# Pairing the layer 1 activations, splitting a weight load, and moving a weight load and the end of a linear-attention kernel

## The chip, the cores and the metric

The kernel runs on one core of one Trainium2 chip. The metric is device time in microseconds (us), the median of several runs. The engines are named as in the profile: PE is TensorE (PEld its weight loads), DVE is VectorE, ACT is ScalarE, POOL is GpSimd, SP is SyncE, which here issues DMAs. A label such as L177 is line 177 of that kernel's file; the change shifts the lines a little, so L178 of the kernel before is L177 of the changed one.

## The reference, cut to what matters

```python
def phi(x):                                   # elu(x) + 1
    return np.where(x > 0, x, np.exp(x) - 1.0) + 1.0
q_p, k_p = phi(q), phi(k)                     # q, k, v: 8 batches x 8 heads x 576 x 64, fp32
kv  = np.einsum('bhsd,bhse->bhde', k_p, v)
z   = np.sum(k_p, axis=2)
num = np.einsum('bhsd,bhde->bhse', q_p, kv)
den = np.einsum('bhsd,bhd->bhs', q_p, z)[..., None] + 1e-06
x   = (num / den) as 4608 tokens x 512
h   = x @ w_in                                # 512 x 2048     "layer 1"
out = (h - np.tanh(h)) @ w_out                # 2048 x 512     "layer 2"
```

## The kernel before

The 4608 tokens are cut into nine tiles of 512. In each tile `c`, layer 1 makes 16 blocks `fi` of 128 x 512 (four matmuls each), ACT takes the tanh and DVE subtracts it into `gT`; layer 2 then takes 16 steps of four matmuls. The attention of the next batch is threaded between these steps by two tables: `s1[fi]` lists what is emitted after block `fi` of layer 1, and `s2[s]` what is emitted after step `s` of layer 2. Each engine is given its instructions in the order in which they are emitted, and in the traces read here no instruction of DVE, ACT or POOL was seen to overtake another: DVE of the changed kernel, for one, starts `prepare`, which needs nothing of q of batch 1, at 39.17 us, after the second `qp` at 38.50 us that waited for it.

```python
def l1act(fi, h, gT):
    th = mpool.tile([128, 512], F32, name="th")            # mpool: bufs=3
    nc.scalar.activation(th, h, AF.Tanh)
    nc.vector.tensor_sub(gT[:, fi, :], h, th)

def gate(gT, fi):                                          # POOL waits here, then issues loads
    g0 = rpool.tile([1, 1], BF16, name="g0")
    nc.gpsimd.tensor_copy(g0, gT[0:1, fi, 0:1])

# loads, all issued from POOL, fp32 in HBM to bf16 on chip, in this order
...                                                        # q, k, v of batch 0
for g in range(4):
    load_wi(g)                                             # 512 columns of w_in each
load_k(1)
load_wo(0)
load_q(1)
...                                                        # memsets
load_wo(1)
load_v(1)
load_wo(2)
...
# first tile (c == 0): attention of batch 1 beside layer 2
s2[0].append(lambda: a_qphi(1, 0))                         # needs q of batch 1
s2[1].append(lambda: (a_qphi(1, 1), load_q(2), load_wo(3), load_k(2), load_v(2)))
s2[4].append(lambda: a_qT_pe(1, 0, side))                  # transposes of qp on PE
s2[5].append(lambda: a_qT_pe(1, 1, side))
s2[5].append(lambda: (b0_scale_rest(side), prepare()))     # DVE
s2[6].append(lambda: a_kv(1, side))                        # 36 small matmuls on PE
s2[8].append(lambda: a_den(1, side))
s2[9].append(lambda: (num1(), a_split(1)))
s2[11].append(lambda: (spread1(0), a_qphi(2, 0)))          # scales of xT for the next tile
s2[13].append(lambda: (spread1(1), a_qphi(2, 1), a_qT_dma(2)))
s2[15].append(lambda: (a_kphi(2, 0), a_vp(2, 0, nc.gpsimd), a_vp(2, 1, nc.gpsimd)))
...
if c >= 1 and n2 < B:                                      # loads of the batch after next
    s1[0].append(lambda: (gate(gT, 0), load_k(n2), load_q(n2), load_v(n2)))
```

`ps_all` is the memory into which the matmuls write (PSUM), here eight banks of 128 x 512. `side` hands out four of these banks in turn. `b0_scale_rest` does four small matmuls into one of them (the "rest" matmuls), and a DVE multiplication (the "rest scale") that frees the bank; `prepare` is nine small DVE instructions that make selection matrices. From the second tile on, `1/den` takes a way round by HBM: SP writes `rden` to `ds` and reads it back, spread over partitions, as `rdb`; DVE needs `rdb` to write `xT` in layer 2.

## Time and profile before

| | before |
|---|---|
| median of 6 runs beside the changed kernel | 295.31 us (295.28 to 295.72) |
| span of the profiled run (first to last instruction) | 293.7 us |
| PE busy / DVE / ACT | 97% / 63% / 51% |
| mean granted PE clock | 0.997 |
| longest PE wait for a load | 1.70 us, for part 1 of `w_out` |

The prediction below shows the lines of this profile on which it rests. A line of the group view reads: line, engine, operation, output <- input, shape, count | busy us in all, mean ns of one | idle time of the engine just before them and what ended it. Two groups are shown here because the change is to halve their number:

```profile
L373 DVE TENSOR_TENSOR gT<-ps_all,th 128x512 bf16<-128x512 f32 x144 | 96.5, 687 | 46.7 <-ACT th L372 46.0
L372 ACT ACTIVATE th<-ps_all 128x512 f32<-128x512 f32 x144 | 85.3, 597 | 48.1 <-PE ps_all L367 42.2
```

Both engines are mostly idle before these instructions, waiting for PE, so they are not what limits the kernel.

### The profile page before, as it was taken

The numbers are of one execution on the slowest core, as the hardware profiler recorded it, in microseconds if no ns is written. First come the engines' busy times: TensorE is split into PE (matmuls) and PEld (weight loads), VectorE is DVE, ScalarE is ACT, GpSimd is POOL, SyncE is SP. The second block draws the span as 40 slices with busy tenths as digits, with TensorE's granted clock in tenths as the row PEclk, the third lists the DMA queues.
The fourth block names the chain that finished last, engine by engine and source line by source line (L and its number), as shares of the span: only waits on it lengthen the run. The fifth ranks groups of instructions, "written<-read, shape, count | busy, mean of one in ns | idle before, by whom it ended". The sixth has DMA issues, their size and how long they took to land.

```text
span 293.7 us, 4685 instructions
## 1 busy us (share of the span) xinstructions
PE 285.4 (97%) x1801; PEld 134.1 (46%) x1801; DVE 183.9 (63%) x326; ACT 150.6 (51%) x233; POOL 34.6 (12%) x55
## 2 busy tenths in 40 slices
PE   8999799999999999999999999999999999999994
PEld 2544364444444444544444445444444444444443
DVE  4759857996578665775578557955780478008600
ACT  4948717766355654555356535752561166136411
POOL 8562030420030002000020003000000000000000
PEclk9999999999999999999999999999999999999998
DMA  7999999897969765957797769787117310130033
GB/s 104 193 205 214 206 206 211 178 186 151 215 119 208 154 142 117 192 120 173 149 152 147 179 138 144 120 203 143 38 34 167 71 37 0 41 85 19 2 71 71
DMA packets 38534, 38.95 MB, mean 133 GB/s; under 512 B 16304, under 2 KB 33264, under 8 KB 37744
## 3 DMA queue, kind: packets, MB, share of 16 engines
q0 software_dynamic: 17008, 18.35, 38.2%
q1 hardware_dynamic: 21424, 20.27, 30.9%
q8 instruction: 14, 0.23, 0.3%
q14 instruction: 8, 0.07, 0.1%
q10 hardware_dynamic: 80, 0.03, 0.0%
HBM read 43.91 MB, written 9.55 MB: 182 GB/s over the span
## 4 chain that ended last, share of the span: by engine, by line
PE 81%; DMA 9%; DVE 5%; POOL 3%; issue 1%; ACT 0%; DVEq 0%; POOLq 0%
PE ps_all L382 39%; PE ps_all L367 35%; DMA w_out_sb<-in_moe_w_out_dram 5%; DMA w_in_sb<-in_moe_w_in_dram 4%; PE ps_all L318 2%; PE ps_all L200 2%; DVE gT L373 1%; PE ps_all L575 1%; DVE xT L360 1%; PE ps_all L277 1%; DVE r L136 1%; DVE kp L137 1%; POOL v L409 1%; PE ps_all L178 1%; DVE qp L137 1%
## 5 line engine op out<-in xcount | busy, mean ns | idle before, releaser
L382 PE MATMUL ps_all<-w_out_sb,gT 128*128 128x512 bf16 x560 | 128.2, 379 | 1.7 <-DMA w_out_sb<-in_moe_w_out_dram 1.7
L367 PE MATMUL ps_all<-xT,w_in_sb 128*128 128x512 bf16 x576 | 128.1, 379 | 0.4 <-DMA w_in_sb<-in_moe_w_in_dram 0.4
L373 DVE TENSOR_TENSOR gT<-ps_all,th 128x512 bf16<-128x512 f32 x144 | 96.5, 687 | 46.7 <-ACT th L372 46.0
L372 ACT ACTIVATE th<-ps_all 128x512 f32<-128x512 f32 x144 | 85.3, 597 | 48.1 <-PE ps_all L367 42.2
L367 PEld LDWEIGHTS <-w_in_sb 128*128 128x128 bf16 x576 | 55.2, 98 | 66.8 <-issue 0.9
L382 PEld LDWEIGHTS <-gT 128*128 128x128 bf16 x560 | 53.9, 98 | 65.9 <-issue 2.1
L388 ACT COPY osb<-ps_all 128x512 f32<-128x512 f32 (+2 forms) x37 | 21.2, 574 | 76.5 <-PE ps_all L382 59.8
L329 DVE TENSOR_TENSOR xT<-ps_all,rdb 128x512 bf16<-128x512 f32 x24 | 16.5, 690 | 14.2 <-PE ps_all L318 14.2
L135 ACT ACTIVATE e<-qraw 128x1152 bf16<-128x1152 bf16 x16 | 18.5, 1163 | 4.6 <-DMA qraw<-in_q_dram 4.6
L137 DVE TENSOR_TENSOR kp<-e,r 128x1152 bf16<-128x1152 bf16 x15 | 12.1, 809 | 12.5 <-ACT e L135 11.6
L135 ACT ACTIVATE e<-kraw 128x1152 bf16<-128x1152 bf16 x15 | 17.4, 1163 | 0.2 <-DMA kraw<-in_k_dram 0.2
L137 DVE TENSOR_TENSOR qp<-e,r 128x1152 bf16<-128x1152 bf16 x16 | 12.1, 758 | 7.9 <-ACT e L135 7.1
L378 POOL COPY g<-gT 1x1 bf16<-1x1 bf16 x5 | 0.9, 179 | 108.4 <-DVE gT L373 108.4
L318 PE MATMUL ps_all<-qT,kz 128*128 128x512 bf16 x28 | 10.1, 379 | 0.0
L434 PE MATMUL ps_all<-zero 128*128 128x512 bf16 x29 | 8.8, 466 | 1.2 <-DVE zero L396 1.2
L136 DVE TENSOR_SCALAR r<-qraw 128x1152 bf16<-128x1152 bf16 x16 | 7.3, 455 | 1.9 <-DMA qraw<-in_q_dram 1.9
L200 PE MATMUL ps_all<-vp,kp 64*128 64x136 bf16 x216 | 7.6, 220 | 0.2 <-DVE kp L137 0.2
L136 DVE TENSOR_SCALAR r<-kraw 128x1152 bf16<-128x1152 bf16 x15 | 7.7, 514 | 0.0
L200 PEld LDWEIGHTS <-kp 64*128 64x128 bf16 x216 | 6.4, 94 | 2.9 <-issue 2.5
L286 DVE RECIPROCAL rden<-den 128x144 f32<-128x144 f32 x7 | 7.4, 1053 | 0.2
L93 POOL DMA_DIRECT2D qraw<-in_q_dram x7 | 5.2, 748 | 14.7 <-DVE r L136 12.3
L93 POOL DMA_DIRECT2D kraw<-in_k_dram x7 | 5.3, 752 | 4.3 <-issue 1.6
(80 smaller groups left out, 105.3 us busy)
## 6 DMA issues: line engine op xcount, KB each, us to landing
out_dram<-osb SPq DMA_DIRECT2D x70, 128.0 KB
rdb<-ds SPq DMA_DIRECT2D x12, 576.0 KB
kraw<-in_k_dram POOLq DMA_DIRECT2D x7, 576.0 KB, 5.9
qraw<-in_q_dram POOLq DMA_DIRECT2D x7, 576.0 KB, 8.0
v<-in_v_dram POOLq DMA_DIRECT2D x7, 576.0 KB, 10.8
w_in_sb<-in_moe_w_in_dram POOLq DMA_DIRECT2D x8, 256.0 KB, 11.7
w_out_sb<-in_moe_w_out_dram POOLq DMA_DIRECT2D x4, 512.0 KB, 14.3
qraw<-in_q_dram POOLq DMA_DIRECT2D x2, 288.0 KB, 4.4
```

The lines of the kernel that those rows point to most:

```text
L93: nc.gpsimd.dma_start(out=t.rearrange("q h i j d -> q (h i) (j d)"), in_=x.rearrange("(n q) x -> q n x", n=4))
L135: return (lambda: nc.scalar.activation(e, x, AF.Exp), lambda: nc.vector.tensor_scalar(r, x, 0.0, 1.0, ALU.max, ALU.add), lambda: nc.vector ...
L136: lambda: nc.vector.tensor_scalar(r, x, 0.0, 1.0, ALU.max, ALU.add),
L137: lambda: nc.vector.tensor_tensor(y, e, r, ALU.min))
L200: nc.tensor.matmul(ps[hg][:, i, :], kp[r, i, j].rearrange("p h d -> p (h d)"), vp[r, i, j, :], start=(j == 0), stop=(j == J - 1))
L318: nc.tensor.matmul(ps, kz[:, p // 2, p % 2, 0:128], qT[:, p % 2, 0:8, p // 2, :], start=True, stop=True)
L329: nc.vector.tensor_mul(xT[:, p, S * b:S * b + 512].rearrange("p (j t c) -> p j t c", j=8, t=4), ps.rearrange("p j (t c) -> p j t c", t=4), ...
L367: nc.tensor.matmul(h, w_in_sb[:, 2 * (p % 2) + p // 2, fi * 128:(fi + 1) * 128], xT[:, p, c * 512:(c + 1) * 512], start=(n == 0), stop=(n ...
L372: nc.scalar.activation(th, h, AF.Tanh)
L373: nc.vector.tensor_sub(gT[:, fi, :], h, th)
L382: nc.tensor.matmul(o, gT[:, fi, i * 128:(i + 1) * 128], w_out_sb[:, fi, :], start=(fi == 0), stop=(fi == NF - 1))
L388: nc.scalar.copy(osb[:, f0:f1], o[:, f0:f1])
```

## The change

The intent is fourfold: fewer instructions on ACT and DVE (activations over two blocks at once from the second tile on), no wait for part 1 of `w_out` (its load goes ahead of q of batch 1, and the work that needs q1 moves to later steps), an earlier first matmul (256 columns of `w_in` in a load of their own), and a shorter end (the last eviction by DVE, its stores over two queues).

```diff
-    mpool = ctx.enter_context(tc.tile_pool(name="mpool", bufs=3))
+    mpool = ctx.enter_context(tc.tile_pool(name="mpool", bufs=2))
+    def l1act2(fi, h, gT):
+        th = mpool.tile([128, 2, 512], F32, name="th")
+        nc.scalar.activation(th, h, AF.Tanh)
+        nc.vector.tensor_sub(gT[:, fi:fi + 2, :], h, th)
 ...
-        nc.scalar.copy(osb[:, f0:f1], o[:, f0:f1])
+        if f0:
+            nc.vector.tensor_copy(osb[:, f0:f1], o[:, f0:f1])
+        else:
+            nc.scalar.copy(osb[:, f0:f1], o[:, f0:f1])
+        last = c == NC - 1 and i == 3          # its second half goes over ACT's queue
 ...
-    for g in range(4):
-        load_wi(g)
+    for f0, n in ((0, 256), (256, 256), (512, 512), (1024, 512), (1536, 512)):
+        load_wi(f0, n)
     load_k(1)
     load_wo(0)
+    load_wo(1)
     load_q(1)
 ...
-    load_wo(1)
     load_v(1)
 ...
-            s2[0].append(lambda: a_qphi(1, 0))
-            s2[1].append(lambda: (a_qphi(1, 1), load_q(2), load_wo(3), load_k(2), load_v(2)))
-            s2[4].append(lambda: a_qT_pe(1, 0, side))
-            s2[5].append(lambda: a_qT_pe(1, 1, side))
-            s2[5].append(lambda: (b0_scale_rest(side), prepare()))
-            s2[6].append(lambda: a_kv(1, side))
-            s2[8].append(lambda: a_den(1, side))
-            s2[9].append(lambda: (num1(), a_split(1)))
-            s2[11].append(lambda: (spread1(0), a_qphi(2, 0)))
-            s2[13].append(lambda: (spread1(1), a_qphi(2, 1), a_qT_dma(2)))
-            s2[15].append(lambda: (a_kphi(2, 0), a_vp(2, 0, nc.gpsimd), a_vp(2, 1, nc.gpsimd)))
+            s2[3].append(lambda: a_qphi(1, 0))
+            s2[4].append(lambda: (a_qphi(1, 1), load_q(2), load_wo(3), load_k(2), load_v(2)))
+            s2[6].append(prepare)
+            s2[7].append(lambda: (b0_scale_rest(side), a_qT_pe(1, 0, side), a_kv(1, side), a_qT_pe(1, 1, side)))
+            s2[9].append(lambda: a_den(1, side))
+            s2[10].append(lambda: (num1(), a_split(1)))
+            s2[12].append(lambda: (spread1(0), a_qphi(2, 0)))
+            s2[14].append(lambda: (spread1(1), a_qphi(2, 1), a_qT_dma(2)))
+            s2[15].append(lambda: a_kphi(2, 0))
 ...                                            # a_vp(2, i), now on DVE, goes to s1[3] of the second tile
-            s1[0].append(lambda: (gate(gT, 0), load_k(n2), load_q(n2), load_v(n2)))
+            s1[1].append(lambda: (gate(gT, 0), load_k(n2), load_q(n2), load_v(n2)))
 ...
-            l1act(fi, h, gT)
+            if c == 0:
+                l1act(fi, h, gT)
+            elif fi % 2:
+                n = dense.order[(dense.n - 1) % 6]
+                l1act2(fi - 1, ps_all[:, n - 1:n + 1, :], gT)
```

More of the change, by code (lines that the diff above doesn't have):

```diff
@@ L105, in load_v, with load_wi @@
         load(b, v_b[b % 2][:, 0:2], v, b == 0)
-    def load_wi(g):
-        f0 = g * (DF // 4)
+    def load_wi(f0, n):
         for h in range(2):
-            nc.gpsimd.dma_start(out=w_in_sb[64 * h:64 * h + 64, :, f0:f0 + DF // 4],
-                                in_=moe_w_in[256 * h:256 * h + 256, f0:f0 + DF // 4].rearrange(
+            nc.gpsimd.dma_start(out=w_in_sb[64 * h:64 * h + 64, :, f0:f0 + n],
+                                in_=moe_w_in[256 * h:256 * h + 256, f0:f0 + n].rearrange(
                                     "(t d) f -> d t f", d=64))
@@ L187, in a_kv, with a_vp @@
             nc.vector.tensor_mul(kz_t[b][:, hg], ps[hg][:, :, 0:160], mask[:, hg])
-    def a_vp(b, i, eng):
-        eng.tensor_copy(vp[:, i, :, 0:128].rearrange("p j (h d) -> p h j d", h=2), v_b[b % 2][:, 0:2, i])
+    def a_vp(b, i):
+        nc.vector.tensor_copy(vp[:, i, :, 0:128].rearrange("p j (h d) -> p h j d", h=2), v_b[b % 2][:, 0:2, i])
     def a_kv_cols(b, banks):
@@ L368, in l1mm @@
                          start=(n == 0), stop=(n == NP - 1))
+    def l1act2(fi, h, gT):
+        th = mpool.tile([128, 2, 512], F32, name="th")
+        nc.scalar.activation(th, h, AF.Tanh)
+        nc.vector.tensor_sub(gT[:, fi:fi + 2, :], h, th)
     def l1act(fi, h, gT):
-        th = mpool.tile([128, 512], F32, name="th")
+        th = mpool.tile([128, 2, 512], F32, name="th")[:, 0, :]
         nc.scalar.activation(th, h, AF.Tanh)
@@ L387, in evac @@
         osb = opool.tile([128, DM], F32, name="osb")
-        nc.scalar.copy(osb[:, f0:f1], o[:, f0:f1])
-        for half, q_ in enumerate((nc.sync, nc.sync if f1 < DM or c < NC - 1 or i < 3 else nc.scalar)):
+        if f0:
[3 more added lines that the diff above has]
+        last = c == NC - 1 and i == 3
+        for half in range(2):
             b, j = divmod(2 * (4 * c + i) + half, J)
-            q_.dma_start(out=out[b * S:(b + 1) * S, f0:f1].rearrange("(p j) m -> p j m", j=J)[:, j, :],
+            (nc.scalar if last and half else nc.sync).dma_start(out=out[b * S:(b + 1) * S, f0:f1].rearrange("(p j) m -> p j m", j=J)[:, j, :],
                               in_=osb[64 * half:64 * half + 64, f0:f1])
@@ L530 @@
             s1[1].append(lambda: a_kphi(2, 1))
+            for i in range(2):
+                s1[3].append(lambda i=i: a_vp(2, i))
         if c >= 1 and n2 < B:
-            s1[0].append(lambda: (gate(gT, 0), load_k(n2), load_q(n2), load_v(n2)))
+            s1[1].append(lambda: (gate(gT, 0), load_k(n2), load_q(n2), load_v(n2)))
             d = 2
@@ L539 @@
             for i in range(2):
-                s2[14 + i].append(lambda i=i: a_vp(n2, i, nc.vector))
+                s2[14 + i].append(lambda i=i: a_vp(n2, i))
         if c == 0:
```

## The prediction

Two of its steps can be read from the profile before. The 1.2 us for the subtraction of a pair: a TENSOR_TENSOR of DVE from `ps_all` and an fp32 tile to bf16 took 415 ns at 128x256 (L264) and 687 ns at 128x512 (L373), so a straight line gives 1231 ns at 128x1024; this is an estimate. And that ACT and DVE do not overtake: in the trace each starts its instructions in the order given, so what waits for a late load holds what stands behind it. POOL likewise issued the load of q of batch 2 only after 12.32 us of waiting for DVE's `r`, and part 3 of `w_out` behind it, at 36.40 and 37.13 us.

> **What bounds the kernel now.** I read the page's busy line first, then who waited for whom, then the timeline. The busy line:
>
> ```profile
> PE 285.4 (97%) x1801; PEld 134.1 (46%) x1801; DVE 183.9 (63%) x326; ACT 150.6 (51%) x233; POOL 34.6 (12%) x55
> ```
>
> TensorE (PE) is the bound; DVE at 63% and ACT at 51% have slack over the whole. What PE waited for (us, times, longest):
>
> ```profile
> PE ps_all L382 <- DMA w_out_sb<-in_moe_w_out_dram: 1.7, 1, 1.7
> ...
> PE ps_all L367 <- DMA w_in_sb<-in_moe_w_in_dram: 0.4, 1, 0.4
> ...
> PE ps_all L200 <- DVE kp L137: 0.2, 1, 0.2
> ```
>
> Only 1.7 us is worth hunting. The chain of waits says the same: from 62.2 us to 289.7 us every piece is PE, a 128x512 matmul each 0.216 us (24 in 5.18). So only the first 62 us and the last 4 can move, and layer-1 activations after 62 us have nothing to give unless they become a wait.
>
> In the first 51 us DMA is saturated; by windows (last column GB/s):
>
> ```profile
> 32.00:34.00 2.00, 2.00 (x11) 0.89 (x10) 2.00 (x4) 0.78 (x2) 0.00 (x0) 1.00 1.24 207
> 34.00:36.00 2.00, 0.44 (x3) 0.10 (x1) 1.27 (x4) 1.76 (x2) 0.00 (x0) 1.00 1.22 208
> ```
>
> Loads land one after another in order of issue. Issue times plus time to landing, issue by issue, give: k of batch 1 at 28.1, w_out 0 at 30.7, q1 33.5, w_out 1 36.1, v1 38.9, w_out 2 41.4, q2 44.3, w_out 3 46.9, k2 49.7, v2 52.5: 2.6 us for 512 KB, 2.8 for 576 KB. The timeline (start, us) around the wait:
>
> ```profile
> 33.55 2.22 ACT L135 ACTIVATE e<-qraw 128x1152 bf16<-128x1152 bf16 x2 [1.23 <-DMA qraw<-in_q_dram]
> ...
> 35.98 0.76 DVE L137 TENSOR_TENSOR qp<-e,r 128x1152 bf16<-128x1152 bf16 x1
> 36.14 1.02 PE L382 MATMUL ps_all<-w_out_sb,gT 128*128 128x512 bf16 x4 [1.70 <-DMA w_out_sb<-in_moe_w_out_dram]
> ...
> 39.41 0.41 DVE L264 TENSOR_TENSOR xT<-ps_all,rdb 128x256 bf16<-128x256 f32 x1
> 39.74 0.70 DVE L481 CAST s<-ident 32x16 f32<-32x16 bf16 x4
> ...
> 39.95 1.66 PE L178 MATMUL ps_all<-v,kp 64*128 64x192 bf16 x36
> ...
> 41.07 0.43 DVE L489 CAST sel<-s 128x512 bf16<-128x512 f32 x1
> ```
>
> q1 is ready for use (qp of both halves) 3.2 us after it lands (33.5 to 36.7). `prepare` (casts to sel) takes 1.76 us on DVE (39.74 to 41.50), here hidden beside the 36 kv matmuls.
>
> [...] 512 rows of 1024 B take 2.57 us, 512 of 1152 B take 2.82. [...] while POOL copies vp (52.6 to 55.4), a DVE instruction of 0.45 us takes 1.40:
>
> ```profile
> 52.97 1.40 DVE L136 TENSOR_SCALAR r<-kraw 128x1152 bf16<-128x1152 bf16 x1
> ```
>
> **The change, part by part.**
>
> *Activations in pairs, from the second tile on.* 128 tanh and 128 subtractions become 64 each. ACT: two of 597 ns become one of about 1.01 us (the 128x1024 copy in the trace took 1.01)[...]. That saves about 64 x 0.18 = 11 us of ACT[...], all of it beside PE: nothing off the time. Risk: from the end of a pair's matmuls to its release is 1.0 + 1.2 = 2.2 us instead of 1.3. Six banks go round in 6 x 0.864 = 5.2 us; a pair takes 1.73 to fill and 2.2 to empty, 3.95 in all, so 1.2 us are left. At the turn to layer 2 the last pair is needed after 14 matmuls, 3.0 us, and ready after 2.2. Both hold, in steady tiles.
>
> *First w_in columns alone.* The first matmuls of layer 1 start at 16.25 after 0.4 us of wait for w_in. Next on PE is the second spread, which starts at 16.77 when DVE's second scale ends at 16.70, whatever w_in does. Gain 0. Cost: the first 512 KB go in rows of 512 B. From 80.3 ns a row and engine at 1024 B (2.57 us / 32) and 88.1 at 1152 B, about 49 ns at 512 B, against 40 for half a row of 1024 B: 64 rows x 9 ns = 0.6 us for all later landings (estimate); I take 0.4.
>
> *w_out 1 ahead of q1.* The queue's bytes are the same. w_out 1 now lands at 33.3 + 0.4, before PE needs it at 34.4: the 1.7 us go. But q1 lands at 36.1 + 0.4. The program's order on each engine then gives (before adding 0.4): steps 4 to 7 of layer 2 run 34.3 to 37.7; the 0.12 us of rest matmuls to 37.85; transposes of q1's first half need qp at 38.1 and end at 38.6; kv needs v1 at 38.9. Its first matmul goes, its second must wait for the bank of the rest matmuls, which is free when DVE has done the rest scale. DVE's order is qp, qp, prepare, rest scale: 36.1 + 3.2 = 39.3, + 1.76 = 41.05, + 0.41 = 41.45. So `prepare`, meant to fill idle DVE time, stands behind the late q1 and in front of what PE waits for: 2.4 us of PE idle. Then kv (1.6) to 43.05 and transposes (0.5) to 43.5, where step 8 starts. Before, step 7 started at 41.54, so step 8 at 42.4: +1.1 us, or +1.5 with the 0.4. PE waits of about 3.0 us replace one of 1.7.
>
> *Turn to the second tile.* The second spread stands three steps before layer 1 instead of four (first: 12 instead of 11; second: 14 instead of 13). Before, spread at 47.41, last xT scale done at 51.74, layer 1 at 51.45 needing it at 52.1: 0.36 us in hand. Now one step of 0.86 fewer is between: about 0.5 us of wait. Then `vp` moves from POOL to DVE (2 x 0.45, behind the second pair). ACT from the end of step 12 (49.5) runs four evictions (2.1), three exp of 1.15 and then tanh, exp, tanh (1.0, 1.15, 1.0), so the second tanh ends at 58.3, the subtraction at 59.5, the first vp copy at 60.0; PE wants it after seven columns at 59.05. Wait about 1.0 us, where there was 0.17. Against that, DVE is no longer held up by POOL's copy (1.7 us in two instructions); that is already in these times.
>
> *End.* The last SP issue goes at about 290.0 instead of 290.53, because the other half of the 384-column piece goes over ACT's queue and DVE does the last eviction. But the ACT queue's piece, issued at 290.01 before, stays where it was, and its packets ended only 0.16 us before SP's last: 0.2 us gained.
>
> *Sum:* 1.1 + 0.4 + 0.5 + (1.0 - 0.2) - 0.2 = +2.6 us, 297.9. After the second tile PE runs without waits, so nothing of it is caught up.
>
> **The rivals.** (1) It gains: the w_out wait goes and q1 is early enough. That makes 295.3 - 1.7 - 0.2 = 293.4. For it: q1's products stand later in the order, so the author gave them room. Against it: q1 moves by 2.6 us in a saturated queue, and DVE's order puts 5.4 us between its landing and the bank that kv wants. (2) Pairs starve PE of banks in every tile: 0.3 us on eight tiles would be +2.4 on top, 300. The 1.2 us in hand and DVE at 63% speak against it. (3) The 2.4 us gap and its neighbours leave PE so idle that the clock is lowered; the 1.7 us gap now does not do it (granted clock 1.00 in all windows)[...]. (4) The waits overlap: a later start of the second tile leaves ACT and DVE to catch up and the 0.5 and 0.8 vanish: 296.6.
>
> **Range and chances.** I shade the sum a little for rival 4 and put 297.6. Low end 295.8: both waits of the turn absorbed and the small rows free. High end 299.2: rivals 2 or 3 in part. 2% is 5.9 us; PE's own work forbids so large a gain, and a loss needs bank starvation in all tiles.
>
> **What would show it.** Right: no PE wait for w_out at 34 us; q1 landing near 36.4; a PE wait of over 2 us at the kv matmuls (line 177), named DVE xT of line 263, near 39 to 42 us; layer 1 of the second tile starting near 52.9 instead of 51.45; a wait for vp (line 189) near 59; from there the PE chain without gaps as before. Wrong: q1 landing before 34.5, the kv matmuls without a wait, or PE waiting for gT (line 373) in tile after tile.

## The result, and the profile after

| | before | after |
|---|---|---|
| median of 6 runs each | 295.31 us | 300.02 us (299.07 to 300.27) |
| ratio | | 1.0152, 95% interval 1.0137 to 1.0167 |
| span of the profiled run | 293.7 us | 298.5 us |
| mean granted PE clock in it | 0.997 | 0.994 |

A ratio in this document is the mean time of one kernel's fast runs over that of the other's in the same rounds, so it is not quite the ratio of the medians. The changed kernel is 1.5% slower, outside the predicted range: 2.4 us above the predicted time and 0.8 us above the top of the range. The loss is real: the slowest of the runs before is 295.72 us and the fastest after is 299.07 us.

The page of the changed kernel, its busy line, its clock in 40 slices of 7.46 us, and the two groups:

```profile
PE 287.7 (96%) x1801; PEld 135.1 (45%) x1801; DVE 175.4 (59%) x265; ACT 139.8 (47%) x168; POOL 33.3 (11%) x55
...
PEclk9999988999999999999999999999999999999999
...
L373 DVE TENSOR_TENSOR gT<-ps_all,th 128x1024 bf16<-128x1024 f32 x64 | 77.9, 1218 | 60.2 <-ACT th L372 60.2
L372 ACT ACTIVATE th<-ps_all 128x1024 f32<-128x1024 f32 x64 | 65.5, 1024 | 58.4 <-PE ps_all L366 48.5
```

ACT is busy 10.8 us less, for 11 us expected, and DVE 8.5 us less: a pair takes 1024 and 1218 ns, where two single ones took 1194 and 1374. PE has the same 1801 matmuls but is busy 2.3 us *more* (287.7 against 285.4). The same work at the same clock should take about as long; the two slices marked 8 in the clock row say where to look, 37 to 52 us.

What PE waited for (us in all, times, longest), and then its timeline in layer 2 of the first tile (start us, us, what, and in brackets the idle time before it and what ended it):

```profile
PE ps_all L177 <- DVE xT L263: 2.6, 1, 2.6
...
PE ps_all L199 <- DVE vp L189: 0.8, 1, 0.8
PE ps_all L317 <- DVE xT L328: 0.6, 1, 0.6
```

```profile
31.14 7.08 PE L387 MATMUL ps_all<-w_out_sb,gT 128*128 128x512 bf16 x32
...
38.99 0.25 PE L177 MATMUL ps_all<-v,kp 64*128 64x192 bf16 x1 [0.16 <-DMA v<-in_v_dram]
41.85 2.02 PE L177 MATMUL ps_all<-v,kp 64*128 64x192 bf16 x35 [2.61 <-DVE xT L263]
...
44.73 2.71 PE L387 MATMUL ps_all<-w_out_sb,gT 128*128 128x512 bf16 x8
```

The wait for `w_out` is gone: 32 matmuls of layer 2 run in one piece where there was a 1.70 us hole. A hole of 2.61 us stands 3 us later, and it is the one predicted. But the eight matmuls after it take 2.71 us; eight of them took 1.90 us in the kernel before. The windows (length, busy us of PE, PEld, DVE, ACT and POOL with counts, granted clock, DMA share, GB/s) tell why:

```profile
40.00:42.00 2.00, 0.15 (x4) 0.15 (x5) 1.89 (x8) 0.00 (x0) 1.89 (x3) 1.00 0.85 95
42.00:44.00 2.00, 2.00 (x38) 1.70 (x35) 0.35 (x2) 0.00 (x0) 0.00 (x0) 0.74 1.19 200
44.00:46.00 2.00, 2.00 (x12) 1.19 (x11) 1.09 (x3) 0.69 (x1) 0.00 (x0) 0.50 1.16 180
46.00:48.00 2.00, 2.00 (x24) 0.84 (x23) 0.14 (x1) 0.00 (x0) 0.00 (x0) 0.90 1.21 202
```

About 1.1 us after the hole PE falls to half clock. In shorter windows the clock reads 0.97 from 42.5 to 43.0 us, 0.50 from 43.0 to 46.0, 0.62 from 46.0 to 46.5 and 1.00 after that, so it is half from 42.97 to 46.38 us. These 3.4 us at half clock leave 1.7 us of work undone. Before, the same windows show 1.00.

Where the 4.8 us of the span came from, by following the start of each stage in both traces:

| stage | after minus before | what was added in the stage before it |
|---|---|---|
| layer 2 of tile 0 starts | +0.3 us | first loads landed 0.2 us later; from -0.1 to +0.8 in the other runs, so not of the change |
| layer 1 of tile 1 starts | +3.1 | -1.70 (`w_out`), +2.61 (kv), +0.16 (v), +1.7 (clock) |
| layer 2 of tile 1 starts | +4.1 | +1.0: waits for the `xT` scales and for `vp` |
| layer 2 of tile 4 starts | +4.2 | nothing but 0.1 |
| layer 1 of tile 5 starts | +5.0 | +0.8: a wait for `rdb` |
| end of the last matmul | +5.0 | nothing |
| end of the span | +4.8 | -0.2: the new end |

The last line of the waits above belongs to tile 4. In the timeline there, DVE stands idle 1.29 us for the broadcast of `1/den`, and PE stands behind it:

```profile
173.75 1.89 DVE L328 TENSOR_TENSOR xT<-ps_all,rdb 128x512 bf16<-128x512 f32 x3 [1.29 <-DMA rdb<-ds]
174.50 0.38 PE L317 MATMUL ps_all<-qT,kz 128*128 128x512 bf16 x1 [0.63 <-DVE xT L328]
```

Why is `rdb` late, from the second tile on, where PE ran without waits before? The gate that opens a tile's loads moved. These are POOL's lines in tile 3, first of the kernel before, then of the changed one:

```profile
115.31 0.18 POOL L378 COPY g<-gT 1x1 bf16<-1x1 bf16 x1 [27.61 <-DVE gT L373]
115.80 0.75 POOL L93 DMA_DIRECT2D kraw<-in_k_dram  x1 [0.31 <-issue]
```

```profile
121.28 0.18 POOL L383 COPY g<-gT 1x1 bf16<-1x1 bf16 x1 [27.61 <-DVE gT L373]
121.77 0.74 POOL L93 DMA_DIRECT2D kraw<-in_k_dram  x1 [0.31 <-ACT th L372]
```

Layer 1 of tile 3 starts at 112.80 us before and at 116.94 us after, 4.1 us later; the loads start 6.0 us later. The gate reads the first block of `gT`, which is now written by the instruction for a pair, so it waits for two blocks of matmuls and for the longer tanh and subtraction. The loads sit 1.8 us deeper in the tile. SP's writes of `rden` to `ds` do not seem to complete until these loads are through: in the ten pairs that I compared (five tiles in each kernel), `rdb` is issued between 0.2 us before and 0.8 us after v of that tile has landed (landing taken as issue plus time to landing), for instance at 158.6 us before (v at 158.1) and 164.4 us after (v at 163.9). In the last tile that needs `rdb`, where no loads run, it is issued 2.4 us after the write of `ds`. SP's lines in tile 4, first before, then after:

```profile
155.05 1.30 SPq L306 DMA_DIRECT2D ds<-rden  x4
158.59 1.13 SPq L309 DMA_DIRECT2D rdb<-ds  x2
```

```profile
159.35 1.30 SPq L305 DMA_DIRECT2D ds<-rden  x4
164.41 1.13 SPq L308 DMA_DIRECT2D rdb<-ds  x2
```

In this tile `rdb` follows the write of `ds` by 3.5 us before and by 5.1 us after. What holds the four writes of 4.5 KB so long is not shown: `rdb` follows v's landing, and no run here took the loads away to prove the cause. Nor is a late issue the whole of the loss: e3 below keeps the moved gate and issues `rdb` in tile 4 as late (5.0 us after the write of `ds`), yet its PE lost only 0.04 us from tile 3 to tile 6. In the changed kernel the broadcast then took 9.3 us to reach DVE, in e3 at most 8.1 us; why that differs is open.

### The profile page after: what moved, and what is told of

It is laid out like the page before. It is cut to its first block, busy times and chain, and to the rows that moved or that the text cites. A ratio compares the mean times of both kernels' runs of the same rounds, so it can differ in the third digit from the quotient of the medians.

```text
span 298.5 us, 4501 instructions
## 1 busy us (share of the span) xinstructions
PE 287.7 (96%) x1801; PEld 135.1 (45%) x1801; DVE 175.4 (59%) x265; ACT 139.8 (47%) x168; POOL 33.3 (11%) x55
## 4 chain that ended last, share of the span: by engine, by line
PE 72%; DMA 17%; DVE 5%; issue 1%; ACT 1%; SPq 1%; POOL 1%; DVEq 0%; POOLq 0%
PE ps_all L366 34%; PE ps_all L387 32%; DMA qraw<-in_q_dram 5%; DMA w_in_sb<-in_moe_w_in_dram 3%; DMA rdb<-ds 3%; PE ps_all L199 2%; DMA out_dram<-osb 2%; DMA kraw<-in_k_dram 2%; PE ps_all L317 2%; DMA ds<-rden 1%; DVE qp L136 1%; DVE xT L359 1%; PE ps_all L276 1%; DVE gT L373 1%; PE ps_all L177 1%
## 5 line engine op out<-in xcount | busy, mean ns | idle before, releaser
L373 DVE TENSOR_TENSOR gT<-ps_all,th 128x1024 bf16<-128x1024 f32 x64 | 77.9, 1218 | 60.2 <-ACT th L372 60.2
L372 ACT ACTIVATE th<-ps_all 128x1024 f32<-128x1024 f32 x64 | 65.5, 1024 | 58.4 <-PE ps_all L366 48.5
L396 ACT COPY osb<-ps_all 128x512 f32<-128x512 f32 (+1 forms) x36 | 20.9, 583 | 73.1 <-PE ps_all L387 49.7
L136 DVE TENSOR_TENSOR kp<-e,r 128x1152 bf16<-128x1152 bf16 x15 | 11.4, 758 | 7.6 <-ACT e L134 6.7
L378 DVE TENSOR_TENSOR gT<-ps_all,th 128x512 bf16<-128x512 f32 x16 | 10.3, 685 | 2.4 <-ACT th L377 1.7
L377 ACT ACTIVATE th<-ps_all 128x512 f32<-128x512 f32 x16 | 9.2, 598 | 4.3 <-PE ps_all L366 3.1
```

What stands on the lines that cost most here:

```text
L136: lambda: nc.vector.tensor_tensor(y, e, r, ALU.min))
L373: nc.vector.tensor_sub(gT[:, fi:fi + 2, :], h, th)
L396: nc.scalar.copy(osb[:, f0:f1], o[:, f0:f1])
```

## The experiments

All kernels were correct. Each had its own runs of the kernel before on the same chip, with medians from 295.02 to 295.29 us.

| label | what it is | median us (runs) | ratio to before |
|---|---|---|---|
| e1_prepare_first | after, `prepare` four steps earlier | 298.36 (6) | 1.0110 |
| e2_spin_in_gap | after, matmuls on zeros in the kv gap | 298.52 (4) | 1.0115 |
| e3_q1_first | after, old order of loads | 296.65 (6) | 1.0054 |
| e5_q1_first_vp_pool | e3, `vp` on POOL as before | 296.28 (4) | 1.0041 |
| e4_pairs_only | before, with the pairs alone | 296.27 (6) | 1.0035 |
| e6_pairs_gate_early | e4, first two blocks single, gate as before | 295.43 (4) | 1.0006 |
| e7_end_only | before, with the new end alone | 295.07 (4) | 0.9996 |
| e8_w_in_only | before, with the `w_in` split alone | 295.14 (5) | 1.0002 |
| e9_prepare_wo3_first | e1, and part 3 of `w_out` ahead of q2 | 295.58 (6) | 1.0021 |
| e10_repaired | e9, rest scale early too, gate as before | 295.25 (5) | 1.0009 |
| e11_turn_earlier | e10, den to spreads one step earlier | 294.47 (4) | 0.9980 |
| c1_reordered | before, new order of loads, DVE order repaired | 293.40 (4) | 0.9940 |
| c2_reordered_pairs | c1 with pairs from the third tile on | 293.65 (5) | 0.9950 |

### Is it DVE's order, and is it the clock?

The theory: `prepare` stands between q1's products and the rest scale, and makes the kv gap; the gap then costs a second time because the clock falls. The rival: the gap costs its own length only.

**e1_prepare_first** takes `prepare` out of the way:

```diff
-            s2[6].append(prepare)
+            s2[2].append(prepare)
```

> The changed kernel with `prepare` put on DVE before the activation of q of batch 1. Theory (DVE's order makes the bank of the kv matmuls late, and the idle time that comes of it halves PE's clock for 3.4 us): the kv wait falls from 2.6 us to under 0.8, the clock stays at 1.00, so about 2.1 + 1.7 = 3.8 us are gained: about 296.2 us. Rival (the lower clock has nothing to do with that idle time): only the wait goes, about 297.9 us, and the clock still drops near 43 us.

Measured: 298.36 us (297.66 to 299.62). The wait at kv fell and the clock stayed at 1.00 after it:

```profile
39.38 1.64 PE L177 MATMUL ps_all<-v,kp 64*128 64x192 bf16 x35 [0.39 <-DVE xT L263]
...
47.80 1.02 PE L387 MATMUL ps_all<-w_out_sb,gT 128*128 128x512 bf16 x4 [1.26 <-DMA w_out_sb<-in_moe_w_out_dram]
```

So `prepare` was the cause of the gap: 2.61 us became 0.39 us. By its time alone this run looks like the rival (297.9 us); the trace decides, where the clock did not drop. Only half of the gain arrived, because two other waits took its place. One is in the second line, 1.26 us for part 3 of `w_out`. Layer 1 of tile 1 nevertheless starts 2.7 us earlier than in the changed kernel (+0.5 us against before, where that had +3.1). The other is at `rdb`, 1.3 us in two tiles (0.8 us in the changed kernel); the last matmul ends at +2.8 us. One of the six runs, the longest at 299.62 us, has a mean clock of 0.994 like the changed kernel; the other five have 0.998 to 1.000. So the clock does not behave alike in every run of one kernel. The trace of that run was not kept, so where its clock fell is not known.

**e2_spin_in_gap** leaves the gap's length and fills it with work whose result nobody reads:

```diff
-  ... (b0_scale_rest(side), a_qT_pe(1, 0, side), a_kv(1, side), a_qT_pe(1, 1, side)))
+  ... (b0_scale_rest(side), a_qT_pe(1, 0, side), spin7(11), a_kv(1, side), a_qT_pe(1, 1, side)))
```

where `spin7(n)` is `n` matmuls of zeros, 128x512, into the bank that kv takes next.

> The changed kernel with 11 matmuls on zeros (0.216 us each, 2.4 us) in the gap ahead of the kv matmuls, into a bank that kv starts anew. No wait is shortened. Theory (idle PE lowers the clock): the clock stays at 1.00 and 1.7 us come back, about 298.3 us. Rival (the drop has another cause, or zeros do not count): no gain, about 300.0 us.

Measured: 298.52 us (298.33 to 298.75), 1.5 us faster than the changed kernel, with 11 matmuls *added*. The same windows as above:

```profile
40.00:42.00 2.00, 1.46 (x17) 0.74 (x17) 1.72 (x8) 0.00 (x0) 1.59 (x3) 1.00 0.95 126
42.00:44.00 2.00, 2.00 (x39) 1.67 (x35) 0.84 (x3) 0.39 (x1) 0.00 (x0) 1.00 1.19 195
44.00:46.00 2.00, 1.95 (x24) 0.85 (x23) 0.44 (x3) 0.30 (x1) 0.00 (x0) 1.00 1.18 191
```

PE is busy in most of the gap (0.54 us stay idle) and the clock stays at 1.00, where it was 0.74 and 0.50; all four runs have mean clocks of 0.997 to 1.000. From the start of layer 2 of the first tile to the start of the next tile this trace takes 22.02 us, the changed kernel's 23.46 us: 1.4 us less, free of what the runs differ by before and after. The rival expected 300.0 us. This is the one experiment that separates the clock from the gap, and it gives the clock 1.5 us, against the 1.7 us worked out from the windows.

**e3_q1_first** undoes the order of the loads alone, with everything else as changed:

```diff
     load_wo(0)
-    load_wo(1)
     load_q(1)
     ...
+    load_wo(1)
```

> The changed kernel with q of batch 1 ahead of the second part of w_out again, all else as changed. Theory (q1's late landing is what makes the kv wait): q1 lands near 33.4 us, the 1.7 us wait for w_out is back at 34 us, the kv wait and the clock drop are gone: about 297.0 us. Rival (the new places of the side work are at fault, whatever the loads): a kv wait of over 1.5 us stays and the time is 299 us or more.

Measured: 296.65 us (296.01 to 298.12), 3.4 us faster than the changed kernel. q1 landed at 33.2 us, there is no wait at kv, the clock stays at 1.0, and the old wait is back as 1.34 us. So of the four parts of the change, moving the load is the one that costs most, and a later q1 is the cause of the gap and of the fall of the clock. The gate is still the moved one here, and the profiled run, the shortest of the six, has almost no wait at `rdb`: the moved gate does not cost it every time.

### The turn to the second tile

**e5_q1_first_vp_pool** is e3 with the copies of `vp` given back to POOL at step 15.

> The kernel of e3 (changed, q of batch 1 ahead of the second part of w_out; 296.65 us, 0.8 us of PE wait for vp) with the vp copies of batch 2 on POOL again. Theory (the vp wait comes from DVE's full queue at the turn to the second column tile): the wait at line 199 for vp goes, DVE loses some of it to POOL, net about -0.5 us: 296.1 us. Rival (any place for vp costs the same, as POOL holds up DVE): within 0.2 us of e3.

Measured: 296.28 us (295.87 to 296.65), against 296.65 us for e3 with overlapping ranges. The wait for `vp` went, and another came, in tile 1:

```profile
57.62 1.02 PE L366 MATMUL ps_all<-xT,w_in_sb 128*128 128x512 bf16 x4 [0.64 <-DVE gT L373]
```

While POOL copies, DVE's instructions are long (`r` 1.43 us, `qp` 1.51 us, where those after it take 0.45 and 0.76; in the kernel before POOL copies from 52.59 to 55.37 us, and `r` takes 1.40 and `kp` 1.51 there), so a subtraction comes late and PE waits for the bank. The medians differ by 0.4 us, which the ranges do not settle.

**e11_turn_earlier** keeps `vp` on DVE and restores one step of lead for the scales of `xT`. It is built on e10, below:

```diff
-            s2[9].append(lambda: a_den(1, side))
-            s2[10].append(lambda: (num1(), a_split(1)))
-            s2[12].append(lambda: (spread1(0), a_qphi(2, 0)))
-            s2[14].append(lambda: (spread1(1), a_qphi(2, 1), a_qT_dma(2)))
+            s2[8].append(lambda: a_den(1, side))
+            s2[9].append(lambda: (num1(), a_split(1)))
+            s2[11].append(lambda: (spread1(0), a_qphi(2, 0)))
+            s2[13].append(lambda: (spread1(1), a_qphi(2, 1), a_qT_dma(2)))
```

> e10 (295.25 us; it was forecast at 294.5 and lost 1.06 us against the kernel before in layer 1 of the second column tile) with denominator, numerator and both spreads one step earlier, where the kernel before has them. Theory (the spreads that stand three steps ahead of layer 1 instead of four push DVE's and ACT's work into the second tile: that is the whole loss at the turn): the waits for the xT scale (0.3) and most of that for vp (0.8) go, 294.1 us. Rival (the vp copies on DVE are the loss, wherever the spreads stand): a vp wait of over 0.6 us stays, 294.9 us or more.

Measured: 294.47 us (294.34 to 294.51), 0.78 us faster than e10 and between the theory (294.1) and the rival (294.9). The wait for the scales is gone and that for `vp` has shrunk from 0.85 to 0.62 us, so each was right in part.

So the 1.0 us of the turn has two parts. The step of lead that was taken is about 0.7 us of it, and the copies on DVE are most of the remainder.

### The pairs and the gate

**e4_pairs_only** puts the pairs, the smaller pool and the moved gate into the kernel before, and nothing else.

> The kernel before with the pairs alone: tanh and subtraction by two tiles from the second column tile on, the gate of the loads after the first pair. Theory (pairs cost PE nothing, but the gate opens 1.2 to 1.9 us later and can make the broadcast of the reciprocals late): 295.3 to 296.2 us, any wait of PE at line 318 for DVE behind that broadcast. Rival (pairs starve PE of PSUM banks): a wait of layer 1 or layer 2 for gT in most column tiles, 297 us or more.

Measured: 296.27 us (295.69 to 296.60), 0.35% slower, which is 1 us, just above what the theory allowed. The prediction gave this part nothing. The waits that the kernel before did not have:

```profile
PE ps_all L318 <- DVE xT L329: 0.4, 1, 0.4
PE ps_all L367 <- DVE gT L374: 0.4, 1, 0.4
```

The first is the wait behind `rdb`; DVE stood idle for it four times, 4.5 us in all, of which only the last part reached PE. By the starts of the stages PE lost 0.3, 0.6 and 0.2 us in layer 2 of tiles 3, 4 and 5, most of it in pieces too short for the list of waits.

**e6_pairs_gate_early** is e4 with the first two blocks of each tile single, so that the gate can stand after the first block again:

```diff
-            if c == 0:
+            if c == 0 or fi < 2:
                 l1act(fi, h, gT)
```

with the line of the gate back at `s1[0]`.

> The kernel of e4 (kernel before plus pairs, 296.27 us) with the first two column tiles of layer 1 singly, so that the gate of the loads opens after the first tile again. Theory (the late gate makes the loads of the next batch collide with the broadcast of the reciprocals): no PE wait at line 318 for DVE behind the broadcast, about 1 us back: 295.3 us. Rival (the pairs themselves delay DVE and with it the reciprocals): 296.0 us or more, waits of line 318 as in e4.

Measured: 295.43 us (295.18 to 295.45), ratio 1.0006 with an interval of 0.9993 to 1.0019. PE has no wait for `xT` of line 329 any more, and from tile 2 on its stages start within 0.02 us of those of the kernel before. Seven of eight pairs in each tile are still there. So what costs 0.8 us is not the pairs as such, but most likely the loads that start later because of them. This edit also makes one pair single, so it doesn't exclude that the very first pair of a tile costs something by itself; the missing `rdb` wait makes the gate the likelier reading. No run moved the gate alone.

### The two small parts

**e7_end_only** is the kernel before with the new end.

> The kernel before with the change of the last tile's end alone. Theory: SP's last issue comes 0.5 us earlier, but the piece on ACT's queue stays where it was: 0.2 us gained, 295.1 us. Rival (the last issue on SP is all that counts): 0.5 us, 294.8 us.

Measured: 295.07 us (294.82 to 295.33), ratio 0.9996 with an interval of 0.9983 to 1.0009: nothing that the times can tell from zero. In the trace, the stretch from the last matmul to the end of the span is about 0.2 us shorter, as predicted. The time is inconclusive.

**e8_w_in_only** is the kernel before with `w_in` in five loads.

> The kernel before with the first w_in columns as DMAs of their own, nothing else. Theory (PE's second spread waits for DVE at 16.7 us whatever w_in does, and short rows cost next to nothing: w_out landings moved by less than 0.2 us): 295.2 to 295.5 us. Rival (short rows delay all landings by 0.4 us, as predicted): the wait for w_out grows to about 2.1 us, 295.7 us.

Measured: 295.14 us (294.87 to 295.48), ratio 1.0002. Part 1 of `w_out`, which comes after all of `w_in` in the queue, landed at 36.11 us (36.10 before, 35.9 to 36.2 in e4, e6 and e7, which have no split). The rows of half length cost nothing that can be seen, where the prediction had taken 0.4 us, and the split gains nothing, as it had said.

### Can the changed order be repaired?

**e9_prepare_wo3_first** is e1 with part 3 of `w_out` issued up front, ahead of the load of q2. The load of q2 waits for a buffer that q1 has to leave; in the changed kernel POOL stood 14.48 us until DVE's `r` of q1 was done and issued it at 38.92 us, and part 3, which stood behind it, at 39.66 us (37.13 before).

> The kernel of e1 (changed, `prepare` first; 298.36 us, 1.3 us of wait for w_out part 3) with part 3 of w_out issued ahead of q of batch 2. Theory (part 3 was late because its issue stood behind a load that waits until q1 has left its buffer): that wait goes, 297.1 us. Rival (DMA's rate is the limit, part 3 lands late anyway): a wait of over 0.8 us for w_out stays, 298 us or more.

Measured: 295.58 us (295.04 to 296.65), 2.8 us faster than e1 (2.6 us by the ratios, as the two ran on different chips), more than expected. Part 3 lands at 43.8 us and PE no longer waits for it; layer 1 of tile 1 now starts 0.9 us *earlier* than in the kernel before. All of this and more is given back later in the profiled run, which is the longest of the six: 1.0 us at the turn, as in the changed kernel, and 1.3 us at `rdb`, in two tiles. The other five runs took 295.04 to 295.76 us; they have no trace, but may well lack the wait at `rdb`, as that of e3 does.

**e10_repaired** moves the rest scale forward as well, and puts the gate back by two single blocks as in e6:

```diff
-            s2[2].append(prepare)
-            s2[7].append(lambda: (b0_scale_rest(side), a_qT_pe(1, 0, side), a_kv(1, side), a_qT_pe(1, 1, side)))
+            s2[2].append(lambda: (b0_scale_rest(side), prepare()))
+            s2[7].append(lambda: (a_qT_pe(1, 0, side), a_kv(1, side), a_qT_pe(1, 1, side)))
```

> The changed kernel with all four suspected causes taken out: `prepare` and the rest scale ahead of q1's activation, part 3 of w_out ahead of q2, the gate after a first single tile. Theory (they are the whole loss): left are the waits of 0.3 us for the xT scale and 0.8 us for vp at the turn, so 293.4 (c1) + 1.1 = 294.5 us. Rival (something else in the changed kernel still loses, pairs for one): 295.3 us or more.

Measured: 295.25 us (294.76 to 295.67), a miss for my theory of 294.5 us and in favour of the rival. It starts tile 1 earlier than the kernel before by 1.06 us and loses all of it at the turn: the scales cost about 0.63 us (the first 28 matmuls took 6.84 us, in e11 6.21 us) and `vp` 0.85 us, not the smaller sum that I had allowed. After that it stays level, with no wait at `rdb`. That miss led to e11.

**c1_reordered** starts from the kernel before instead. It takes the new order of the loads and the new end, leaves the activations single and the `vp` copies on POOL, and orders DVE's work so that nothing independent stands behind q1:

```diff
     load_wo(0)
+    load_wo(1)
     load_q(1)
 ...
-    load_wo(1)
     load_v(1)
     load_wo(2)
+    load_wo(3)
 ...
-            s2[0].append(lambda: a_qphi(1, 0))
-            s2[1].append(lambda: (a_qphi(1, 1), load_q(2), load_wo(3), load_k(2), load_v(2)))
-            s2[4].append(lambda: a_qT_pe(1, 0, side))
-            s2[5].append(lambda: a_qT_pe(1, 1, side))
-            s2[5].append(lambda: (b0_scale_rest(side), prepare()))
-            s2[6].append(lambda: a_kv(1, side))
+            s2[1].append(lambda: (b0_scale_rest(side), prepare()))
+            s2[2].append(lambda: a_qphi(1, 0))
+            s2[3].append(lambda: (a_qphi(1, 1), load_q(2), load_k(2), load_v(2)))
+            s2[7].append(lambda: (a_qT_pe(1, 0, side), a_kv(1, side), a_qT_pe(1, 1, side)))
```

> A repaired version on the kernel before (single activations): w_out parts 1, 2 and 3 issued without waiting for q of batch 1, w_out 1 ahead of q1; rest scale and `prepare` on DVE ahead of q1's activation; the side work of q1 and kv after step 7; the new end. Theory (of the changed kernel only the order on DVE and the buffer wait of the next loads lose time): no wait for w_out over 0.4 us, waits of about 0.3 us each for qp, v and w_out 2, clock at 1.00, about 1.2 us gained: 294.0 us. Rival (the first 50 us are bound by DMA, any order pays the same): 295 us or more.

Measured: **293.40 us** (293.36 to 293.48), ratio 0.9940 with an interval of 0.9925 to 0.9954: better than the 294.0 us expected. It beats both kernels, though by less than 2% it counts as the same. PE's timeline in layer 2 of the first tile:

```profile
32.89 5.34 PE L382 MATMUL ps_all<-w_out_sb,gT 128*128 128x512 bf16 x23
...
38.67 1.66 PE L178 MATMUL ps_all<-v,kp 64*128 64x192 bf16 x36
...
41.16 1.02 PE L382 MATMUL ps_all<-w_out_sb,gT 128*128 128x512 bf16 x3 [0.23 <-DMA w_out_sb<-in_moe_w_out_dram]
```

The 36 kv matmuls run in one piece without a wait, and all that is left of the waits for `w_out` is 0.23 us. Tile 1 starts at 50.20 us instead of 51.45 us. Another 0.64 us are gained in layer 1 of tile 1 (15.56 us instead of 16.20 us), whose cause was not traced, and the new end gives the rest. Which of the changes in order earns how much was not separated.

**c2_reordered_pairs** adds pairs from the third tile on to c1.

> c1 (293.40 us) with pairs of tanh and subtraction from the third layer-1 tile on and the gate after the first tile. Theory (pairs free ACT and DVE, which PE does not wait for after 60 us): 293.2 to 293.6 us. Rival (the relief of DVE at the turn to the second tile counts): up to 0.4 us faster; or pairs make waits for gT there: 293.8 us.

Measured: 293.65 us (293.14 to 293.90), ratio 0.9950 with an interval of 0.9938 to 0.9961, which overlaps that of c1: the same. Pairs are worth nothing to the time that can be seen, which is what the group lines of the profile before say: ACT and DVE wait for PE, not PE for them.

## Why the prediction was wrong

By its steps:

- **"w_out 1 ahead of q1": right, and close.** No wait for `w_out` near 34 us. q1 landed at 36.05 us (predicted 36.5). DVE's order was qp, qp, `prepare`, rest scale, and kv went on at 41.85 us. The steps give 41.45, or 41.85 with the 0.4 us added; that it fell on the second is partly luck. The 0.4 us for short rows did not come, but `prepare` took 2.30 us instead of 1.76: its first four casts took 1.24 us, while POOL was issuing loads, for 0.70 in the kernel before and 0.69 in e1, where POOL was not; whether that is the cause was not tested. The chain of waits of the changed kernel (start us, us, what) shows it as the steps had it, with `sel` the last instruction of `prepare`:

```profile
38.50 0.76 DVE qp L136
...
41.04 0.07 DVE sel L498
...
41.38 0.42 DVE xT L263
...
41.85 2.02 PE ps_all L177 x35
```

  The wait was 2.61 us for 2.4 predicted. Without the clock, layer 2 of tile 0 lost 3.14 - 0.31 - 1.71 = 1.1 us, for 1.1 predicted. e1 and e3 confirm the two causes, `prepare` and q1.
- **"the 1.7 us gap now does not do it" (rival 3): the first step that failed.** The rival was named, and then left out of the sum, which priced the gap by its length alone, and given only part of the top of the range. The clock fell to half for 3.4 us and cost 1.7 us by the windows, 1.5 us by e2. The gap before the change was 1.70 us and its clock was 1.00; the step from there to 2.61 us was taken as safe without any measurement between. The six runs of the changed kernel have mean clocks of 0.993 to 0.994 in five, at 299.77 to 300.27 us, and 0.997 in the shortest, at 299.07 us, which is inside the predicted range. The kernel before has 0.997 to 1.000 too, so that run probably kept its clock.
- **"all of it beside PE: nothing off the time" and "After the second tile PE runs without waits": the second step that failed.** The busy time saved is right (1024 ns for a pair on ACT, 1010 predicted, and 1218 on DVE, 1.2 us predicted), and the count of banks held. What was overlooked is a line of the diff beside it: the gate moved from `s1[0]` to `s1[1]`. The loads started 1.8 us deeper in the tile, `rdb` came late, and 0.8 us was lost in tile 4. e4 shows about 1 us from this part alone and e6 shows it gone with the gate back. How much of it a run pays varies (e3).
- **"First w_in columns alone": gain right, cost wrong.** No gain, but no 0.4 us either (e8). Its estimate from row sizes had no measurement below 1024 B.
- **"Turn to the second tile": right in kind, a little large.** 0.5 + 0.8 = 1.3 us predicted, 1.0 us measured; e11 confirms that both waits are there. Rival 4, that the two vanish, did not happen.
- **"End": right by the trace** (0.2 us), too small for the times (e7).

The sum was +2.6 us, shaded to +2.3. Measured by the traces: 1.1 + 1.0 - 0.2 = 1.9 us for the steps that were named, 1.7 for the clock, 0.8 for the late `rdb`, 0.1 between the turn and tile 4 and 0.3 of start, which is chance: 4.8 us. The size of the `rdb` term, too, is that of one run.

What stays open: how long a gap PE can have before the clock falls. In the 3.41 us before PE went on, a stretch as long as the slow one after it, it had worked 0.65 us in the changed kernel and 1.71 us in the kernel before, whose clock held; no run lies between, and e1 lost clock in one run of six, while the trace of another of its runs has no gap of over 1.3 us. It is also open in which tile the wait for `rdb` falls and how long it is, which differs from kernel to kernel (0.04 us in the trace of e3, 0.8 in the changed kernel, 1.3 in e1 and e9, all with the moved gate); and by what the loads hold SP's writes, if they do.

## What to carry to other kernels

Before moving a load back in a queue that is as busy as this one (207 to 208 GB/s, a load of 512 KB or 576 KB every 2.6 to 2.8 us; q1 landed at 36.05 us instead of 33.5), follow its consumers on every engine that was seen to keep its order: independent work queued behind it (`prepare` on DVE, part 3 of `w_out` in POOL's issue order) becomes late with it, and the version that emits that work *ahead* of the wait, with the loads in the new order, was the fastest here (293.40 us). When activations are merged, look for what else read the first of them: a gate on it moves too, and shifts every transfer that it opens (by 1.8 us in the tile here). And price an idle gap of PE with the clock that may fall after it, not only with its length: here 2.61 us of gap were followed by 3.4 us at half clock, which cost 1.5 to 1.7 us, and 11 matmuls on zeros in the gap kept the clock at 1.00 (e2).
